# Attention of one query over a long cache: the last three tiles in another order

## Chip, cores, metric

The kernel runs on one core of a Trainium2 chip. The metric is device time in microseconds (us), lower is better. Executions of one kernel on one chip lie within about 0.3% of each other.

## The reference

For 256 heads (batch 8 x 32) one query of 128 numbers meets 4096 keys and values, all in bf16:

```python
B, H, Sq, Skv, Dh = 8, 32, 1, 4096, 128
scores = jnp.einsum('bhqd,bhkd->bhqk', q, k) * scale
attn = _softmax(scores, axis=-1)
return jnp.einsum('bhqk,bhkd->bhqd', attn, v)
```

K and V are 537 MB together and each byte is used once, so the load of K and V is the floor.

## The kernel before

The heads are done in 32 tiles of 8 heads. A tile has 8 MB of K and 8 MB of V: 128 partitions x 256 columns (`C`) x 128 numbers. It goes in quarters (`Q` = 64 columns) through these steps (PE is the matmul engine, TensorE; VectorE, ScalarE and GpSimd are the other compute engines; PSUM is the buffer that the matmuls write to; DMA brings K and V in):

- `product`: VectorE multiplies K by the query and adds the two halves (L170, L173 in the profile).
- `sum_over_d`: PE adds up the rest by matmuls with an identity (L185).
- `scores_of`: VectorE reads the sums from PSUM (L197); `weights_of`: VectorE finds the maximum and a bias (L218), ScalarE takes exp (L230).
- `values_of`: PE multiplies the weights with V (L246), one tile later, because V of a tile is loaded after its K.
- `norm_of` (PE L259, VectorE L264), `copy_of` (ScalarE L270), `result_of` (PE L279) finish two tiles.

Below, "sums" are the matmuls of `sum_over_d` (8 to a quarter), and "values" those of `values_of` (4 columns each, so 16 to a quarter). Expectations and text call PE "warm" when it has its full clock.

K and V share three buffers. V of tile t goes into the buffer of K of tile t, K of tile t+1 into that of V of tile t-2.

```python
    for t in range(NT):
        ...                                    # loads, product(t, 0, Q), rest of values(t-2), copy
        product(t, Q, 2 * Q)
        sum_over_d(t, 1)
        scores_of(t, 0)
        if t > 1:
            if t % R == 1:
                norm_of(t // R - 1)
            result_of(t - 2)
        if t > 0:
            values_of(t - 1, 0, Q)             # V of t-1 may still be under way
        product(t, 2 * Q, 3 * Q)
        sum_over_d(t, 2)
        scores_of(t, 1)
        if t > 0:
            values_of(t - 1, Q, 2 * Q)
        product(t, 3 * Q, C)
        sum_over_d(t, 3)
        scores_of(t, 2)
        scores_of(t, 3)
        weights_of(t)
        if t > 0:
            values_of(t - 1, 2 * Q, 3 * Q)
    values_of(NT - 2, 3 * Q, C)
    copy_of(NT - 2)
    norm_of(NQ - 1)                            # waits for the last exp of tile 31
    result_of(NT - 2)
    values_of(NT - 1, 0, C - LAST)
    copy_of(NT - 1)
    result_of(NT - 1)                          # 4 matmuls, then LAST small ones straight from V
```

The last exps are done in two halves of columns, so half of the last weights are ready early; in front of `values_of(31)` that is of no use as long as `norm_of` stands there.

## Time and profile before

| | before |
|---|---|
| time, median of 3 runs | 1270.92 us |
| span of the profiled run (first to last instruction) | 1270.8 us |
| DMA over the span | 423 GB/s |
| last bias (VectorE, tile 31) starts | 1240.12 us |
| from there to the end of the span | 30.7 us |

A first thing to read is when the load is over. This is the table of stretches of the kernel before; columns: stretch, its length, busy us (and instructions) of PE, weight loads, VectorE, ScalarE, GpSimd, then the granted PE clock, the busy share of the DMA engines, and GB/s.

```profile
1244.00:1245.00 1.00, 1.00 (x6) 0.42 (x5) 0.00 (x0) 1.00 (x7) 0.00 (x0) 1.00 1.06 426
...
1246.00:1247.00 1.00, 0.00 (x0) 0.00 (x0) 0.00 (x0) 1.00 (x5) 0.00 (x0) 1.00 0.71 287
...
1248.00:1249.00 1.00, 0.00 (x0) 0.00 (x0) 0.00 (x0) 1.00 (x7) 0.00 (x0) 0.62 0.23 94
1249.00:1250.00 1.00, 0.16 (x2) 0.15 (x3) 0.18 (x1) 1.00 (x5) 0.00 (x0) 0.50 0.05 20
1250.00:1251.00 1.00, 0.79 (x7) 0.49 (x6) 0.17 (x2) 0.21 (x1) 0.00 (x0) 0.50 0.00 0
```

DMA is full until 1246, runs dry over the next four us and has ended at 1250. The other 21 us of the span come after the last byte. Also, PE does nothing from 1246 to 1249 and is then granted half its clock.

Why PE was late is to be seen earlier. This is the timeline of the kernel before in tile 30; columns: start, duration, engine, line, operation, result and inputs, shapes, count, and in brackets the engine's idle time before it and who ended it.

```profile
1182.20 0.09 PEld L246 LDWEIGHTS <-w 128*32 128x32 bf16 x1
1184.98 2.29 DVE L173 TENSOR_TENSOR kt<-kt 128x4096 bf16<-128x4096 bf16 x1
...
1191.36 6.40 PE L246 MATMUL av<-vt,w 128*32 128x512 bf16 x16 [9.09 <-DMA vt<-in_v_dram]
...
1197.69 1.90 PE L185 MATMUL ps<-kt,ident 128*128 128x512 bf16 x8
...
1199.63 0.69 DVE L197 TENSOR_REDUCE sc<-ps 128x64 f32<-128x512 f32 x1 [5.10 <-PE ps L185]
...
1203.08 1.90 PE L185 MATMUL ps<-kt,ident 128*128 128x512 bf16 x8
...
1205.02 0.69 DVE L197 TENSOR_REDUCE sc<-ps 128x64 f32<-128x512 f32 x1 [4.70 <-PE ps L185]
```

VectorE had the third quarter of the product ready at 1187.27 (1184.98 + 2.29). Its sums run at 1197.69. What stands between them on PE is 16 values that wait 9.09 us for V. The Trainium skill ("TensorE: Matmul & The Clock Gate", Part 2, Step-by-step) says that matmuls stay in program order and only weight loads may be pulled ahead. The trace agrees: the weights of the blocked value were loaded at 1182.20, 9 us before it could run, and the sums with ready inputs stayed behind it. VectorE then waits 5.10 and 4.70 us for sums, so the next tile starts late.

The end of the kernel before, from the chain of waits (start, duration, engine, tile or line):

```profile
1240.38 9.40 ACT w L230 x32
1249.78 0.43 ACT comb L270
...
1250.26 0.58 PE op L279 x4
1250.84 15.17 PE av L246 x60
...
1266.04 0.59 ACT comb L270
...
1268.08 0.36 ACT stage L294
```

And two lines of the timeline, the last bias and the second part of the norm:

```profile
1240.12 0.23 DVE L218 TENSOR_SCALAR bias<-own,nmax 128x8 f32<-128x8 f32 x1
...
1249.84 0.21 PE L259 MATMUL zp<-ones,late 128*16 128x1 f32 x2 [4.33 <-ACT w L230]
```

The exps of the last tile end at 1249.8, PE has waited 4.33 us for them in `norm_of`, and only then do 60 matmuls with values begin, although nearly all of V has landed and half of the weights have been ready for about 4.5 us.

### The profile page before, as it was taken

Reading aid. Unit: us, or ns where it says so; the run is one execution under the profiler, and the core shown is the slowest. Engines: PE = TensorE matmul, PEld = TensorE weight load, DVE = VectorE, ACT = ScalarE, POOL = GpSimd, SP = SyncE. Lnnn points to the kernel's source line nnn. Section 1 sums busy time; section 2 is a strip of 40 time slices with the busy share of each in tenths; the row PEclk is TensorE's granted clock in tenths of the full one; section 3 lists DMA queues with packets and bytes.
Section 4 is the critical chain, followed back from the end, with each engine's and each line's share of the span. In section 5 each row is a group of like instructions: output and inputs, shape, how many; then the busy total and the mean of one; then the engine's idle time right before and its main releaser. Section 6 shows DMA issues by size and latency. Waiting matters only on the chain.

```text
span 1270.8 us, 8147 instructions
## 1 busy us (share of the span) xinstructions
PE 837.4 (66%) x3310; PEld 326.2 (26%) x3310; DVE 968.7 (76%) x532; ACT 341.1 (27%) x641; POOL 2.8 (0%) x16
## 2 busy tenths in 40 slices
PE   2476766657666768667677567686665776586667
PEld 0122322222222223222222222232222222232223
DVE  5987787776878777876878867788787788967690
ACT  0323123322133231233321332312332213332033
POOL 0000000000000000000000000000000000000000
PEclk9688977888878888788888787888788978888898
DMA  9999999999999999999999999999999999999992
GB/s 398 452 425 426 435 430 433 438 432 430 433 434 432 428 438 432 437 430 433 440 430 428 431 430 435 426 438 433 432 434 435 439 430 418 433 434 429 415 424 113
DMA packets 12742, 537.53 MB, mean 423 GB/s; under 512 B 1952, under 2 KB 1952, under 8 KB 2208
## 3 DMA queue, kind: packets, MB, share of 16 engines
q1 hardware_dynamic: 12096, 536.88, 98.0%
q8 instruction: 26, 0.43, 0.1%
q10 hardware_dynamic: 608, 0.13, 0.0%
q14 instruction: 12, 0.10, 0.0%
HBM read 536.94 MB, written 0.07 MB: 423 GB/s over the span
## 4 chain that ended last, share of the span: by engine, by line
DMA 61%; DVE 20%; PE 17%; ACT 1%; issue 0%; DVEq 0%
DMA kt<-in_k_dram 54%; DVE kt L170 13%; PE ps L185 9%; PE av L246 8%; DVE kt L173 7%; DMA vt<-in_v_dram 6%; DMA q_all<-in_q_dram 1%; ACT w L230 1%; DVE sc L197 0%; DVEq L170 0%; PE qh L154 0%; ACT comb L270 0%; PE op L285 0%; PE op L279 0%; DVE pmax L207 0%
## 5 line engine op out<-in xcount | busy, mean ns | idle before, releaser
L170 DVE TENSOR_TENSOR kt<-kt,qb 128x8192 bf16<-128x8192 bf16 x128 | 565.1, 4415 | 136.9 <-DMA kt<-in_k_dram 124.7
L246 PE MATMUL av<-vt,w 128*32 128x512 bf16 x2044 | 526.9, 417 | 112.6 <-DMA vt<-in_v_dram 112.6
L185 PE MATMUL ps<-kt,ident 128*128 128x512 bf16 x1024 | 298.6, 444 | 274.1 <-DVE kt L173 273.9
L230 ACT ACTIVATE w<-sc,bias 128x256 bf16<-128x256 f32 (+1 forms) x264 | 301.2, 1557 | 624.8 <-DVE bias L218 624.8
L246 PEld LDWEIGHTS <-w 128*32 128x32 bf16 x2044 | 205.7, 104 | 428.8 <-issue 250.3
L173 DVE TENSOR_TENSOR kt<-kt 128x4096 bf16<-128x4096 bf16 x128 | 293.4, 2292 | 4.4
L185 PEld LDWEIGHTS <-ident 128*128 128x128 bf16 x1024 | 105.3, 108 | 466.3 <-issue 348.8
L197 DVE TENSOR_REDUCE sc<-ps 128x64 f32<-128x512 f32 x128 | 87.6, 685 | 97.4 <-PE ps L185 97.4
L230 ACT ACTIVATION_READ_ACCUMULATOR w<-sc,bias 128x1 f32 x264 | 130.8, 496 | 0.0
L270 ACT ACTIVATE comb<-av 32x512 bf16<-32x512 f32 x32 | 19.1, 596 | 233.2 <-PE qh L154 155.8
L160 PE MATMUL qp<-qg,heads 8*128 8x128 bf16 x32 | 6.9, 216 | 24.8 <-ACT qg L158 24.8
L264 DVE RECIPROCAL rz<-zp 16x1 f32<-16x1 f32 x16 | 2.5, 155 | 26.5 <-PE zp L259 26.4
L154 PE MATMUL qh<-q_all,ident 128*8 128x128 bf16 x32 | 7.2, 224 | 13.9 <-DMA q_all<-in_q_dram 13.9
L294 ACT ACTIVATE stage<-op,rz 16x128 bf16<-16x128 f32 x16 | 5.7, 358 | 35.1 <-PE op L279 33.6
L158 ACT ACTIVATE qg<-qh 8x128 bf16<-8x128 f32 x32 | 8.0, 251 | 23.3 <-PE qh L154 23.3
L207 DVE TENSOR_REDUCE pmax<-sc 128x1 f32<-128x256 f32 x32 | 13.4, 420 | 1.1
L279 PE MATMUL op<-comb,pick 32*16 32x128 bf16 x128 | 12.5, 217 | 0.9 <-ACT comb L270 0.9
L162 ACT ACTIVATE qb<-qp 128x128 bf16<-128x128 f32 x32 | 8.9, 277 | 9.7 <-PE qp L160 9.7
L279 PEld LDWEIGHTS <-pick 32*16 32x16 bf16 x128 | 6.8, 84 | 8.0 <-issue 7.6
L209 DVE TENSOR_SCALAR spread<-same,pmax 128x32 f32<-128x32 f32 x32 | 7.7, 241 | 1.1
L218 DVE TENSOR_SCALAR bias<-own,nmax 128x8 f32<-128x8 f32 x32 | 7.4, 230 | 1.1
L160 PEld LDWEIGHTS <-heads 8*128 8x128 bf16 x32 | 2.9, 91 | 20.7 <-issue 20.4
(29 smaller groups left out, 22.1 us busy)
## 6 DMA issues: line engine op xcount, KB each, us to landing
kt<-in_k_dram SPq DMA_DIRECT2D x6, 4096.0 KB, 25.5
kt<-in_k_dram SPq DMA_DIRECT2D x8, 2048.0 KB, 19.4
vt<-in_v_dram SPq DMA_DIRECT2D x4, 2048.0 KB, 17.5
vt<-in_v_dram SPq DMA_DIRECT2D x7, 1024.0 KB, 18.0
vt<-in_v_dram SPq DMA_DIRECT2D x2, 512.0 KB, 18.0
vt<-in_v_dram SPq DMA_DIRECT2D x30, 26.1
kt<-in_k_dram SPq DMA_DIRECT2D x27, 26.2
q_all<-in_q_dram ACTq DMA_DIRECT2D x1, 64.0 KB, 13.0
```

Source lines behind the costliest of these rows:

```text
L158: nc.scalar.activation(out=qg[:], in_=qh[:], func=ACT.Copy)
L160: nc.tensor.matmul(qp[:], lhsT=heads[:].rearrange("g h x -> g (h x)"), rhs=qg[:], start=True, stop=True)
L162: nc.scalar.activation(out=qb[:, 0, :], in_=qp[:], func=ACT.Copy)
L170: nc.vector.tensor_tensor(out=part, in0=part, in1=qb[:].to_broadcast([P, MC, D]), op=ALU.mult)
L173: nc.vector.tensor_tensor(out=part[:, :, 0 : D // 2], in0=part[:, :, 0 : D // 2], in1=part[:, :, D // 2 : D], op=ALU.add,)
L185: nc.tensor.matmul(ps[:], lhsT=ident[:], rhs=kt[:, u * UC : (u + 1) * UC, s * DS : (s + 1) * DS], start=(s == 0), stop=(s == n - 1),)
L197: nc.vector.tensor_reduce(out=scs[t][:, u * UC : (u + 1) * UC], in_=sums.pop((t, u))[:], axis=AX.X, op=ALU.add)
L207: nc.vector.tensor_reduce(out=pmax[:], in_=sc[:], axis=AX.X, op=ALU.max)
L230: nc.scalar.activation(out=w[:, c0 : c0 + n, g], in_=sc[:, c0 : c0 + n], func=ACT.Exp, bias=bias[:, g : g + 1], scale=scale, accum_out=esu ...
L246: nc.tensor.matmul(avs[t][:], lhsT=w[:, c0 : c0 + CB, :], rhs=vt[:, c0 : c0 + CB, :], start=(c0 == 0), stop=(c0 + CB == (C if t < NT - 1 e ...
L270: nc.scalar.activation(out=comb[:], in_=avs.pop(t)[:], func=ACT.Copy)
L279: nc.tensor.matmul(ops[n][:], lhsT=pick[:, m, r, :], rhs=comb[:, m * D : (m + 1) * D], start=(r == 0 and m == 0), stop=(r == R - 1 and m = ...
```

## The change

Its intent: in the last tiles sums must not stand on PE behind values whose V is under way, and at the very end norm and sums must not stand in front of values that could run. `LAST` (columns that skip the copy) goes from 16 to 8, and the small copy of the last weights goes from VectorE to GpSimd.

```diff
-LAST = 16
+LAST = 8
...
-        ("v", NT - 1): [C // 8] * 7 + [C // 16, LAST],
+        ("v", NT - 1): [C // 8] * 7 + [C // 16, C // 32, LAST],
...
-            nc.vector.tensor_copy(out=w_last[:, :, RG - G : RG], in_=w[:, C - LAST : C, :])
+            nc.gpsimd.tensor_copy(out=w_last[:, :, RG - G : RG], in_=w[:, C - LAST : C, :])
...
         for t in range(NT):
+            late_v = t >= NT - 3
...
-            if t > 0:
+            if t > 0 and (t == NT - 1 or not late_v):
                 values_of(t - 1, 0, Q)
             product(t, 2 * Q, 3 * Q)
             sum_over_d(t, 2)
             scores_of(t, 1)
-            if t > 0:
+            if t > 0 and (t == NT - 1 or not late_v):
                 values_of(t - 1, Q, 2 * Q)
...
             if t > 0:
-                values_of(t - 1, 2 * Q, 3 * Q)
+                values_of(t - 1, 0 if late_v and t < NT - 1 else 2 * Q, 3 * Q)
         values_of(NT - 2, 3 * Q, C)
         copy_of(NT - 2)
+        values_of(NT - 1, 0, C // 2)
         norm_of(NQ - 1)
         result_of(NT - 2)
-        values_of(NT - 1, 0, C - LAST)
+        values_of(NT - 1, C // 2, C - LAST)
```

In effect only tiles 29 and 30 change their order; tile 31 keeps it.

## The prediction

> **What bounds the kernel now.** The stretch table shows the DMA engines busy 0.96 to 1.06 of every stretch from 1080 to 1246 us, at 385 to 434 GB/s, then falling from 0.78 to 0.04: the last bytes of V land near 1249.7. Up to there the loads are the bound. The span ends at 1270.8: a tail of 21 us. The timeline shows why: sums over d stand on PE behind values whose V is under way (PE waits 7.6 to 10.4 us for V in tiles 29 to 31), so scores are late: the last bias is ready at 1240.4, the last exp at 1249.8. Norm of the last weights stands on PE ahead of the last values and waits for that exp (4.3 us), so all 60 last matmuls run after the load, 1250.8 to 1266.0; then 16 small ones (1.06 us) and the store.
>
> **What the change does.**
> - Tiles 29 and 30: three quarters of the previous values move behind the fourth sum. PE's work is the same; DVE's waits for sums go (1.4 + 4.7 us in tile 29, 5.1 + 4.7 in tile 30).
> - Half of the last values go ahead of norm; they need only the first half of the exps.
> - LAST 16 to 8: two more matmuls of 0.22 us, eight fewer of 0.066. The small copy (0.20 us on DVE) goes to POOL, off the path. One more DMA.
>
> **Where it lands** (estimate from these durations). A quarter on DVE is 4.42 + 2.29 us. Tile 29's fourth sum ends near 1161.5 instead of 1164.8; 48 values follow, the first seven at the slow clock. The Trainium skill, "TensorE: Matmul & The Clock Gate", Part 1, puts the slow clock after an idle window of about 3.4 us; the trace agrees: 16 matmuls take 6.34 us after a 10 us wait, 3.63 in a busy stretch. V 28's slot comes free near 1178.8 (before: 1178.6), so K 31 is issued no later, 12 us ahead of need. Tile 30's fourth sum: 1195 instead of 1205. Last bias 1229.7; half the exps 1234.5, all 1239.2. V 29's values run 1195 to 1212.5, V 30's, limited by landing, to 1235. Then V 31's: eight matmuls per 1 MB piece take 1.77 us, a piece lands each 2.4 us, so PE catches up near piece 5 and ends about 0.7 us after the last byte, 1250.4. From last value to end was 4.8 us, now 4.3.
>
> **On the critical path.** DMA's end stays near 1249.7: the engines were full already. Only the 21 us behind it can be won, and about 16 are. 1270.8 falls to about 1255.0, 1.2% faster; range 1251.5 to 1260. Faster by over 2% needs under 1245.5, below the DMA end: 0.02. Within 2%: 0.97. Slower: 0.01.
>
> **What would show it.** First V 30 issue near 1195; last bias near 1230; V 31's values interleaved with landings, waiting for DMA, not for norm; last DMA byte still 1249 to 1250; from there to the end about 5 us; one run of 48 values each in tiles 29 and 30.
>
> **What would make it wrong.** The 48 values delaying K 31 by over 10 us; PE at the slow clock during V 31's values, 0.43 us each, slower than the landings: up to 6 us; uneven ends of the DMA engines holding the last pieces; a slow copy on POOL; bandwidth varying between chips: 0.3% is 4 us.

## The result

| | before | after |
|---|---|---|
| time, median (4 runs each) | 1271.06 us | 1256.80 us |
| range | 1269.75 to 1271.21 | 1256.36 to 1257.75 |
| ratio, 95% interval | | 0.9891 (0.9874 to 0.9908) |
| span of the profiled run | 1270.8 us | 1254.9 us |
| last bias starts | 1240.12 us | 1231.13 us |
| from there to the end | 30.7 us | 23.8 us |

Ratios are the mean time of one kernel's fast runs over that of the other's of the same rounds, so not quite the ratio of the medians. The change takes 14.3 us by the medians, 1.1%: faster beyond the noise, and within 2%.

The stretches of the changed kernel at the end:

```profile
1244.00:1245.00 1.00, 1.00 (x6) 0.44 (x5) 0.00 (x0) 0.00 (x0) 0.00 (x0) 1.00 1.00 408
...
1246.00:1247.00 1.00, 1.00 (x7) 0.41 (x5) 0.00 (x0) 0.00 (x0) 0.00 (x0) 1.00 0.72 287
...
1248.00:1249.00 1.00, 1.00 (x6) 0.47 (x5) 0.00 (x0) 0.00 (x0) 0.00 (x0) 1.00 0.19 74
1249.00:1250.00 1.00, 1.00 (x7) 0.47 (x5) 0.00 (x0) 0.00 (x0) 0.00 (x0) 1.00 0.12 29
1250.00:1251.00 1.00, 0.52 (x3) 0.10 (x2) 0.00 (x0) 0.45 (x1) 0.00 (x0) 1.00 0.00 0
```

The load ends as before, at 1250, but PE has no gap and keeps its full clock, and the span ends 5 us after the load instead of 21.

Tile 30 in the timeline of the changed kernel:

```profile
1188.81 2.29 DVE L173 TENSOR_TENSOR kt<-kt 128x4096 bf16<-128x4096 bf16 x1
...
1191.16 3.57 PE L185 MATMUL ps<-kt,ident 128*128 128x512 bf16 x8 [3.69 <-DVE kt L173]
...
1194.66 13.06 PE L246 MATMUL av<-vt,w 128*32 128x512 bf16 x56
...
1194.77 0.69 DVE L197 TENSOR_REDUCE sc<-ps 128x64 f32<-128x512 f32 x1 [3.06 <-PE ps L185]
```

The fourth quarter's sums follow VectorE by 0.06 us and end at 1194.7 (before: 1205.0); the values then run in one piece, 48 of tile 29's and the next eight of the same tile. VectorE's wait for sums in this tile is 3.06 us instead of 5.10 + 4.70. It is not zero: 1.4 us of it is there at full clock too (in tile 31 VectorE waits 1.38 us for the last sums, which take 1.89), and the rest is the slow clock: PE, with less to do in between, has gone to it in the quarter before, and eight sums take 3.57 us instead of 1.89.

The end, from the chain of waits of the changed kernel:

```profile
1227.50 1.89 PE ps L185 x8
1229.39 14.01 PE av L246 x64
1243.40 0.08 PE zp L259 x4
...
1243.79 6.74 PE av L246 x30
...
1250.55 0.60 ACT comb L270
...
1252.15 0.36 ACT stage L294
```

The chain goes through PE without a break from 1227.50 on. The exps (32 ScalarE pieces, 9.4 us of the chain before) and the wait in norm are no longer in it. The first half of the exps is close behind, though: it ends at about 1236.3, and PE is through with V of tile 30 and needs these weights at about 1236.4. Two lines of the timeline of the changed kernel that are needed below, the last bias and the reciprocal of an earlier norm on VectorE in tile 31:

```profile
1213.39 0.16 DVE L264 RECIPROCAL rz<-zp 16x1 f32<-16x1 f32 x1 [2.77 <-PE zp L259]
...
1231.13 0.23 DVE L218 TENSOR_SCALAR bias<-own,nmax 128x8 f32<-128x8 f32 x1
```

### The profile page after: what moved, and what is told of

Read it like the earlier page. It is cut to its first block, busy times and chain, and to the rows that moved or that the text cites. A ratio compares the mean times of both kernels' runs of the same rounds, so it can differ in the third digit from the quotient of the medians.

```text
span 1254.9 us, 8136 instructions
## 1 busy us (share of the span) xinstructions
PE 840.3 (67%) x3304; PEld 326.8 (26%) x3304; DVE 968.6 (77%) x531; ACT 341.3 (27%) x641; POOL 3.0 (0%) x17
## 4 chain that ended last, share of the span: by engine, by line
DMA 58%; DVE 23%; PE 18%; issue 0%; ACT 0%; DVEq 0%
DMA kt<-in_k_dram 55%; DVE kt L170 15%; PE ps L185 9%; PE av L246 8%; DVE kt L173 8%; DMA vt<-in_v_dram 2%; DMA q_all<-in_q_dram 1%; DVE sc L197 0%; ACT comb L270 0%; DVEq L170 0%; PE qh L154 0%; DVE pmax L207 0%; PE op L279 0%; PE op L285 0%; PE zp L259 0%
## 5 line engine op out<-in xcount | busy, mean ns | idle before, releaser
L185 PE MATMUL ps<-kt,ident 128*128 128x512 bf16 x1024 | 303.5, 450 | 275.3 <-DVE kt L173 275.2
L207 DVE TENSOR_REDUCE pmax<-sc 128x1 f32<-128x256 f32 x32 | 13.4, 420 | 1.1
```

What stands on the lines that cost most here:

```text
L185: nc.tensor.matmul(ps[:], lhsT=ident[:], rhs=kt[:, u * UC : (u + 1) * UC, s * DS : (s + 1) * DS], start=(s == 0), stop=(s == n - 1),)
L207: nc.vector.tensor_reduce(out=pmax[:], in_=sc[:], axis=AX.X, op=ALU.max)
```

## The experiments

Two numbers sort all runs: where the last bias starts (what the order inside the tiles decides), and how long it takes from there to the end of the span (what the end decides). "vs before" is the difference of the medians of the same rounds.

| run | time, median | vs before | span | last bias | bias to end |
|---|---|---|---|---|---|
| before | 1271.06 | | 1270.8 | 1240.12 | 30.7 |
| after | 1256.80 | -14.3 | 1254.9 | 1231.13 | 23.8 |
| e1_order_only | 1262.97 | -8.4 | 1260.4 | 1229.14 | 31.3 |
| e2_tail_only | 1263.32 | -8.0 | 1261.8 | 1238.23 | 23.6 |
| e3_last8_only | 1270.47 | -0.9 | 1268.2 | 1238.21 | 30.0 |
| e7_tile30_only | 1259.84 | -11.5 | 1257.7 | 1234.10 | 23.6 |
| a1_changed_again | 1256.54 | -13.4 | 1254.9 | 1230.99 | 23.9 |
| e4_one_tile_more | 1256.80 | -13.1 | 1254.8 | 1229.84 | 25.0 |
| e5_less_v (wrong result) | 1255.86 | -14.1 | 1254.3 | 1230.80 | 23.5 |
| e6_less_v_one_tile_more (wrong) | 1255.45 | -14.5 | 1254.0 | 1230.03 | 24.0 |
| a2_changed_again | 1256.47 | -13.6 | 1254.4 | 1228.91 | 25.5 |
| e8_small_first | 1255.98 | -14.1 | 1253.8 | 1228.55 | 25.3 |
| e9_norm_moved_result_not | 1264.00 | -6.1 | 1262.9 | 1231.42 | 31.5 |
| e10_norm_later_too | 1258.93 | -11.3 | 1257.5 | 1234.41 | 23.1 |

The runs came in four calls, each on one chip (e1, e2, e3, e7; a1, e4, e5, e6; a2, e8, e9; e10), and are compared within a call where less than 1 us matters. e8 and e10 ran on the same chip, with 1270.10 and 1270.22 for the kernel before. The last bias of one and the same kernel differs by up to 2 us between profiles (before's order: 1240.1 and 1238.2; the changed kernel: 1231.1, 1231.0, 1228.9).

### Each half of the change alone

e1_order_only: the changed kernel with the old end.

```diff
-        values_of(NT - 1, 0, C // 2)
         norm_of(NQ - 1)
         result_of(NT - 2)
-        values_of(NT - 1, C // 2, C - LAST)
+        values_of(NT - 1, 0, C - LAST)
```

(and `LAST`, the cuts of the load and the small copy as before)

> The changed order of tiles 29 to 31 alone; the end (norm first, 16 small matmuls, copy of the last weights on VectorE) as before. My theory: the two halves are separate waits, and the gain of each is what it takes off its own wait. Last bias ready near 1231 as in the changed kernel, exps all done at 1240.8, norm then stands idle for 4.4 us ahead of the last values, PE goes to the slow clock, 60 values take 15.2 us from 1241.9: span about 1262, 9 us under before. Rival (the order in the tiles is the whole gain, the end is cosmetic): 14 us or more under before. Rival (norm in front of the values hides the gain): within 2 us of before.

Measured: 8.4 us under before (expected 9), bias to end 31.3 us, as with the old end. Timeline of this run:

```profile
1238.86 0.22 PE L259 MATMUL zp<-ones,late 128*16 128x1 f32 x2 [4.33 <-ACT w L230]
...
1239.79 15.87 PE L246 MATMUL av<-vt,w 128*32 128x512 bf16 x60
```

PE waits 4.33 us in norm again, as before, and the 60 values take 15.87 us. My theory holds, both rivals fall.

e2_tail_only: the kernel before with the new end.

```diff
+        values_of(NT - 1, 0, C // 2)
         norm_of(NQ - 1)
         result_of(NT - 2)
-        values_of(NT - 1, 0, C - LAST)
+        values_of(NT - 1, C // 2, C - LAST)
```

> The new end alone (half of the last values ahead of norm), everything else as before. My theory: last bias stays at 1240.4, exps end at 1249.8, the first 32 values run warm 1245.4 to 1252.5, the other 28 to 1259.4: 6.6 us under before. Rival (without the earlier scores the new end wins nothing): within 1 us of before. Sum of this gain and that of the order alone: about 15.6, if the parts add.

Measured: 8.0 us under before (7.0 by the ratio; expected 6.6); bias to end 23.6 instead of 30.7, that is 7.1 less. Timeline of this run:

```profile
1236.42 14.07 PE L246 MATMUL av<-vt,w 128*32 128x512 bf16 x64
...
1250.81 6.22 PE L246 MATMUL av<-vt,w 128*32 128x512 bf16 x28
```

The trace splits these 7.1: counted from the last bias, the last tile's values begin about 5.4 us earlier (before: 10.65 us after the bias, at 1250.77; here right behind values of tile 30, 64 in one run of 14.07 us), and they run at the full clock, where 60 took 15.23 us before and 28 + 32 take about 13.3 at 0.22 us each. So the slow clock is about 2 of the 7 us (norm and four matmuls, now between the two halves, give 0.3 back).

e3_last8_only: only `LAST` 8, the cuts to match, and the copy on GpSimd.

```diff
-LAST = 16
+LAST = 8
-            nc.vector.tensor_copy(out=w_last[...
+            nc.gpsimd.tensor_copy(out=w_last[...
```

> Only the 8 small matmuls instead of 16, with the load cut to match and the copy of the last weights on GpSimd. My theory: two values of 0.22 us more against eight small ones of 0.066 us less: 0 to 0.2 us under before, not to be told from zero. Rival (the shorter end is a part of the gain): 0.5 us or more under before.

Measured: 0.9996 with an interval of 0.9981 to 1.0011, not to be told from zero. The eight small matmuls take 0.61 us instead of 1.06; 62 values took 15.07 us where 60 had taken 15.23, so the slow clock's phase hides the two extra ones. The copy on GpSimd takes 0.24 us by the profile, off the chain.

As far as the noise lets one see, the parts add: 8.4 + 8.0 + 0.9 = 17.3 by medians (7.6 + 7.0 + 0.5 = 15.1 by the ratios times 1271), against 14.3 (13.9 by the ratio) for the whole. Each ratio is uncertain by about 2 us (0.0015 to 0.0017 of 1271), so 15.1 and 13.9 are not different beyond noise. They add because they lie in series in one chain: the order in the tiles moves the last bias, the end shortens what follows it. Whether the load cuts something off the sum is asked below.

e7_tile30_only: tile 29 back to its old order (`late_v = t >= NT - 2`).

> The changed kernel, but tile 29 in its old order (only tile 30 keeps its sums free of values). My theory: the chain of VectorE from tile 29 on is what counts: tile 29 ends near 1166.7 again, the last bias at 1234.8 instead of 1231.4, and PE behind it ends as much later: 3 to 4 us over the changed kernel, about 10.5 under before. Rival (the loads set the end of the changed kernel with slack to spare): no more than 0.5 us over the changed kernel, 14 under before.

Measured: 3.0 us over the changed kernel (1259.84 against 1256.80; ratios 0.9916 against 0.9891, which is 3.2 us). The last bias starts 3.0 us later, and bias to end is the same, 23.6. As far as can be compared, the time here follows the chain of VectorE.

### Norm, or more than norm

e9_norm_moved_result_not: the changed kernel, but the matmuls that take up the copy of tile 30's sums stay ahead of the last values.

```diff
+        result_of(NT - 2)
         values_of(NT - 1, 0, C // 2)
         norm_of(NQ - 1)
-        result_of(NT - 2)
         values_of(NT - 1, C // 2, C - LAST)
```

> The changed kernel, but the four matmuls that take up the copy of tile 30's sums go back ahead of the last values; norm stays behind half of them. My theory: two things blocked PE in the old end and not one. The copy stands on ScalarE behind all 16 exps of the last tile and ends 0.9 us after the last of them, so PE still stands from the end of V 30's values (about 1236.5) to about 1241.5 and then goes on slow: 6 to 8 us over the changed kernel, as long from last bias to end as before (30 to 31). Rival (norm alone blocked, as the change is described): the changed kernel's time within 0.5 us.

Measured: 1264.00 against 1256.47 on the same chip, 7.5 us over. Timeline of this run, the four matmuls and the values behind them:

```profile
1241.56 0.58 PE L279 MATMUL op<-comb,pick 32*16 32x128 bf16 x4 [4.87 <-ACT comb L270]
...
1242.07 9.91 PE L246 MATMUL av<-vt,w 128*32 128x512 bf16 x32
```

PE now waits 4.87 us for the copy, which stands on ScalarE behind the 16 exps, and then runs at the slow clock (32 values in 9.91 us; warm they take about 7.1). So norm was only one of two things in the way, and with the other left in place the new end wins nothing: bias to end is 31.5 us. The change works because it moves both. The reverse, norm left in front and the four matmuls moved, was not run; that norm would block as well is read from the trace of before, where PE stands in it until 1249.84.

### What ends the changed kernel: the load or the chain?

The chain of the changed kernel holds no DMA from 1160 on, yet it ends close to the load. Four runs on one chip were to tell which of the two sets the end.

> The changed kernel itself, on the chip of the next three runs, to compare them with. All theories: 14 to 16 us under before.

Measured (a1_changed_again, no edit): 1256.54, 13.4 under before, a little less than expected.

e4_one_tile_more: `late_v = t >= NT - 4`.

> The changed kernel with tile 28 in the new order as well, so that the scores of the last four tiles are free of waits for V. Theory of the load (the last bytes of V at about 1250 end it, whatever the scores do): last bias 3 to 5 us earlier, and the time 0 to 0.5 us under the changed kernel. Rival, theory of the chain (from tile 28 on, the chain of waits of the changed kernel holds no DMA, only VectorE and PE): the time follows the bias, 3 to 4 us under the changed kernel.

Measured: 1256.80, no faster. The bias came only 1.15 us earlier than in a1, not 3 to 5. Up to the end of tile 29 the expected size was there: its bias starts at 1158.26, in a1 at 1163.00. Then VectorE waits 3.24 us for K of tile 30, and 0.43 us for K of tile 31 at 1195.69:

```profile
1158.26 0.23 DVE L218 TENSOR_SCALAR bias<-own,nmax 128x8 f32<-128x8 f32 x1
...
1161.73 4.43 DVE L170 TENSOR_TENSOR kt<-kt,qb 128x8192 bf16<-128x8192 bf16 x1 [3.24 <-DMA kt<-in_k_dram]
```

So the tiles cannot start earlier: I had not looked at when K lands. The load, full at that time (426 GB/s from 1155 to 1162), is the limit here too, by way of K and not of V. Whatever it won at the bias is given back in waits for V, as the timeline of this run shows in the last values:

```profile
1242.41 1.90 PE L246 MATMUL av<-vt,w 128*32 128x512 bf16 x8
1244.76 1.89 PE L246 MATMUL av<-vt,w 128*32 128x512 bf16 x8 [0.45 <-DMA vt<-in_v_dram]
...
1247.25 3.18 PE L246 MATMUL av<-vt,w 128*32 128x512 bf16 x14 [0.60 <-DMA vt<-in_v_dram]
```

e5_less_v: the last 1 MB of V is not loaded, its matmuls read the 32 columns before it. Its output is wrong, which doesn't matter for the time.

```diff
-        ("v", NT - 1): [C // 8] * 7 + [C // 16, C // 32, LAST],
+        ("v", NT - 1): [C // 8] * 6 + [C // 16, C // 32, LAST],
...
+            v0 = c0 - C // 8 if t == NT - 1 and c0 >= C - C // 8 else c0
...
-                avs[t][:], lhsT=w[:, c0 : c0 + CB, :], rhs=vt[:, c0 : c0 + CB, :],
+                avs[t][:], lhsT=w[:, c0 : c0 + CB, :], rhs=vt[:, v0 : v0 + CB, :],
...                                                       # small matmuls likewise
```

> Wrong result on purpose: the last 1 MB of V's last tile is not loaded, its matmuls read the 32 columns before it. Theory of the load: 2.4 us (1 MB at 425 GB/s) under the changed kernel. Theory of the chain: no change. My view before the run is a tie, since PE runs without a break from 1229.3 to 1250.5 and the last byte lands at about 1250: 0 to 0.5 us under the changed kernel.

Measured: 0.7 us under a1 (span 0.6; expected 0 to 0.5), bias to end 23.5. The stretches of this run show the load running dry about 2 us earlier (0.17 of the engines busy from 1246 to 1247, against 0.19 from 1248 to 1249 in the changed kernel):

```profile
1246.00:1247.00 1.00, 1.00 (x6) 0.47 (x5) 0.00 (x0) 0.00 (x0) 0.00 (x0) 1.00 0.17 64
1247.00:1248.00 1.00, 1.00 (x7) 0.46 (x5) 0.00 (x0) 0.00 (x0) 0.00 (x0) 1.00 0.00 0
```

and its timeline shows the last values in one run that ends at 1250.03, not 2.4 us earlier:

```profile
1243.38 6.65 PE L247 MATMUL av<-vt,w 128*32 128x512 bf16 x30
```

So in this run the chain sets the end; 2.4 us of load were worth 0.7.

e6_less_v_one_tile_more: both edits.

> Both edits together. Theory of the load: 2.4 us under the changed kernel, as without the fourth tile. Theory of the chain: 3 to 4 us, as with the fourth tile alone. A tie of the two: 2 to 2.5 us here, although each edit alone gives 0 to 0.5.

Measured: 1255.45, 1.1 us under a1. This is more than either edit alone but less than the 2 to 2.5 that I expected of a tie of two: the third limit, K of tiles 30 and 31 landing (VectorE waits 2.18 us for the first at 1161.70 and 0.45 us for the second at 1195.67), stops the chain from moving further. The changed kernel stands where three limits lie within one or two us of each other: VectorE and PE from tile 29 on, the landing of K of tile 30 (in a1 that tile starts at 1163.14, in e4, when K has landed, at 1161.73), and the end of V.

The same kernel run again shows both sides of that tie:

> The changed kernel once more, on the chip of the next two runs, to compare them with. All theories: 13 to 15 us under before; from last bias to the end of the span 23.5 to 24.

Measured (a2_changed_again): 1256.47. In this profile the last bias starts at 1228.91, 2.1 us earlier than in a1, and the span is only 0.5 us shorter. My expected 23.5 to 24 from bias to end was missed (25.5): the rest went into waits for V, and the chain of waits of this profile runs through the DMA of V from 1194.19 to 1246.83.

```profile
1241.92 1.89 PE L246 MATMUL av<-vt,w 128*32 128x512 bf16 x8 [0.20 <-DMA vt<-in_v_dram]
...
1244.41 1.89 PE L246 MATMUL av<-vt,w 128*32 128x512 bf16 x8 [0.60 <-DMA vt<-in_v_dram]
...
1246.87 3.18 PE L246 MATMUL av<-vt,w 128*32 128x512 bf16 x14 [0.58 <-DMA vt<-in_v_dram]
```

### Two attempts to go further

e8_small_first: tile 28 in the new order too, and the small matmuls ahead of the four that wait for the copy.

```diff
-            late_v = t >= NT - 3
+            late_v = t >= NT - 4
...                                  # in result_of: the loop over LAST goes ahead of
...                                  # the loop over CB; stop is set on the last of CB
```

> An attempt at a faster version: tile 28 in the new order too, and at the very end the eight small matmuls ahead of the four that wait for the copy of the sums, so that PE works while ScalarE copies. My theory: the copy takes 0.59 us and the eight small ones 0.61, so they fit behind each other's back: from the start of the copy to the end of the span 0.5 to 0.6 us less than in the changed kernel (4.35 there), and the same in the time. Rival (the last small matmuls wait for the last piece of V, which lands later than the copy ends): no change.

Timeline of this run:

```profile
1249.82 0.61 PE L280 MATMUL op<-vt,w_last 128*16 128x128 bf16 x8
1250.02 0.59 ACT L270 ACTIVATE comb<-av 32x512 bf16<-32x512 f32 x1 [11.35 <-PE av L246]
...
1250.66 0.38 PE L285 MATMUL op<-comb,pick 32*16 32x128 bf16 x4 [0.23 <-ACT comb L270]
```

The small matmuls run before and during the copy. From the start of the copy to the end of the span it is 3.78 us (1253.8 - 1250.02), against 4.31 in a2 (1254.4 - 1250.09): 0.53 less, as expected. The time is 0.5 us lower, 1255.98 against 1256.47; the ranges just fail to touch (1255.52 to 1256.13 and 1256.14 to 1256.72). It is the fastest correct kernel, by a margin that only the trace makes credible.

e10_norm_later_too: in tile 31 of e8 the norm of tiles 28 and 29 one quarter later. The reciprocal of that norm holds up VectorE for 2.2 us in e8 (2.77 in the changed kernel, shown above).

```diff
-            if t > 1:
+            if t > 1 and t < NT - 1:
                 if t % R == 1:
                     norm_of(t // R - 1)
                 result_of(t - 2)
...
             scores_of(t, 1)
+            if t == NT - 1:
+                norm_of(t // R - 1)
+                result_of(t - 2)
```

> The kernel with tile 28 in the new order and the small matmuls first, and in tile 31 the norm of the tiles 28 and 29 (a reciprocal on VectorE, which waits 2.2 to 2.8 us for PE in that place in all the changed kernels) one quarter later, where PE has caught up. My theory: that wait is what made the last bias later than I had predicted; it goes to under 0.3 us, and the last bias comes 2 us or more earlier, at 1226 to 1227 if K lands as there. But the load ends the kernel by then: the values of V 31 wait for V by as much more, and from the last landing to the end nothing changes: time within 0.5 us of the kernel without this edit (about 14 us under before). Rival (the chain of VectorE still sets the end): 2 us less.

Measured: 1258.93, 2.95 us slower than e8 on the same chip. My theory fell. Timeline of this run:

```profile
1215.23 5.27 PE L246 MATMUL av<-vt,w 128*32 128x512 bf16 x16 [3.51 <-DMA vt<-in_v_dram]
...
1222.50 0.16 DVE L264 RECIPROCAL rz<-zp 16x1 f32<-16x1 f32 x1 [5.49 <-PE zp L259]
...
1229.36 3.31 PE L185 MATMUL ps<-kt,ident 128*128 128x512 bf16 x8 [3.02 <-DVE kt L173]
```

One quarter later on PE is behind the first values of tile 30, which wait 3.51 us for V and then run at the slow clock. The reciprocal inherits that: VectorE waits 5.49 us instead of 2.19. I had made the very mistake that the change repairs, putting what VectorE needs behind values whose V is under way. The run is still of use: its bias is 5.9 us later than e8's (1234.41 against 1228.55), and the time only 2.95 later. So in e8 the chain had 2 to 3 us of slack before the load (5.9 - 2.95 by the times, 25.3 - 23.1 by bias to end), and past that the time follows the chain. Whether the norm in an earlier place, ahead of tile 29's values, would free VectorE was not tried; with the load at its end in e8, little is to be expected of it.

## Why the prediction was right

The time lay in the range, and the span was 1254.9 for a predicted 1255.0. Point by point:

- **The load ends at about 1249.7 and does not move**: right, it ends between 1249 and 1250 in both.
- **Only the 21 us behind it can be won, about 16 are**: the tail went from 21 to 5 us; the two profiled spans differ by 15.9. By medians it is 14.3. The 1.8 us between 1255.0 and 1256.8 come from one term: I took the span of one profile as the time. Each run looked at took 1.7 to 1.9 us longer than its own span (the profiled one 1256.61 against 1254.9), and the profiled run of before was a long one (1272.47, against a median of 1270.92), so its span happened to equal the median.
- **Sums of tiles 29 and 30 end near 1161.5 and 1195**: 1161.3 and 1194.7. V of tile 30 was issued at 1194.76, K of tile 31 at 1177.6, no later than before.
- **PE waits for V in tiles 29 to 31, and VectorE's waits for sums go**: partly wrong. The three waits of 7.6 to 10.4 us are in tiles 28 to 30 (10.44, 7.58 and 9.09 us; none in 31), and 3.06 us of wait for sums is left in each of tiles 29 and 30. The dates above were right all the same.
- **Last bias near 1230**: it was ready at 1231.4, predicted 1229.7. What the trace shows at that place is the reciprocal of the earlier norm: it holds VectorE up for 2.77 us in tile 31 (1.51 us before), because PE comes late from its run of 56 values. e10 was to test this and did not, so it is read from the trace and not shown by a run.
- **Values of V 31 interleaved with landings, waiting for DMA**: wrong for the profile of the changed kernel, where PE runs without a wait; right for a2 (waits of 0.20, 0.60 and 0.58 us). The prediction had the load end the last values at 1250.4; in the profile the chain, its last bias 1.7 us late, ended them at 1250.5. That the number fits is luck: the chain and the load end so close to each other that it hardly mattered which came last.
- **Norm blocks the last values**: right, but not all of it. The prediction names norm alone; e9 shows that with norm alone moved its gain at the end would have been nothing. The edit moved both blockers, so the number came out.
- **Values end at 1250.4, tail 4.3**: 1250.5 and 4.4.
- **Slow copy on GpSimd, K 31 delayed, slow clock in the last values**: none happened.

How it works is shown by e1, e2 and e9: two separate waits in series, and in the second, two blockers (that norm alone blocks is read from the trace of before). e4 and e5 show that an earlier order in the tiles or an earlier end of the load alone gives no more than 0.7 us, e6 that both together give 1.1, e8 that 0.5 was left behind the last values.

## What to carry to other kernels

On an engine that works in program order, look for what stands behind a wait, and not at the wait: here sums with ready inputs stood up to 10 us behind values that waited for V, and moving them cost nothing. Before the gain of such a reordering is believed, list everything that stands in front, since norm alone, without the four matmuls that wait for the same exps through another engine, gained nothing. And near a floor ask where the chain, each load's landing and the end of the load lie: when they are within one or two us of each other, a single further edit gains little (0.7 us at most here).

## What the Trainium skill lacked or had wrong

- "TensorE: Matmul & The Clock Gate" (Part 1, HAM oscillation) gives "no PE-idle gaps >~3.4µs" as the rule (about 3 us in the page's closing table). Here an idle gap of 3.02 us left PE at full clock in one run (before, at 1229.23: eight sums in 1.89 us), and the same gap of 3.02 us was followed by the slow clock in another (e10, at 1229.36: 3.31 us). After 3.04 us in the changed kernel, at 1183.90, the eight sums took 3.57; the granted clock was at 0.50 from 1182.75 on, under 2 us after PE's last matmul (1180.86). The page says that the window runs freely, which fits the two outcomes of one gap; that a gap shorter than the window is enough it does not say. The same page's figures for slow and full clock (426.7 and 215.7 ns for 512 columns) agree with the runs: behind a wait of 9 us the weight loads follow each other by 0.43 us (before, from 1191.74 on), and in a busy run 32 values take 7.08 us, 0.22 each.
- "DMA: Bandwidth & Descriptors" (Specifications) lists a limit of about 358 GB/s of HBM per core; this core, with no other core of the program running, moved 428 GB/s over the whole span of the changed kernel. What the table calls a limit is half of what two cores share; "HBM Reference" (Specifications) says so and gives about 425 for a core streaming alone.
- I found no page that tells how a long load runs out: here the DMA engines' busy share fell over about 4 us, from 0.96 to 0.12, at the end of the load (changed kernel, 1245 to 1250). Which of the 16 engines ended last was not looked at.
- "Runtime: NRT & Kernel Launch" (The ~15µs preamble/postamble breakdown) gives a gap of about 6.2 us by which the profile's total time exceeds the reported one. I found no page with the gap that mattered here, by which the time exceeds the span from first to last instruction: 1.7 to 1.9 us in the runs looked at.
